# Attention and a tanh-shrink layer on one core: k and q of pairs 8 to 31 turned by the DMA crossbar, loads of two pairs at a time, a new pattern of layer steps

## The chip, the core and the metric

The kernel runs on one core of a Trainium2 chip. Its five engines are PE (TensorE), DVE (VectorE), ACT (ScalarE), POOL (GpSimd) and SP (SyncE, which here issues nearly all DMAs). The metric is the device time of one execution in microseconds, and the number that is compared is the median of several runs.

## The reference

For each of 8 batches and 8 heads there are q, k and v of 576 rows and 64 columns in float32. The rows of the attention's output, with the heads side by side, then pass a layer of two matrix products with `h - tanh(h)` between them.

```python
scores = (1 / sqrt(64)) * q @ k.T
thresh = max(scores, axis=-1) - tau          # tau = 0.02
scores = where(scores >= thresh, scores, -1e9)
attn = softmax(scores)                       # 1e-9 added to the sum
x = (attn @ v), heads side by side           # 4608 x 512
h = x @ w_in                                 # 512 x 2048
out = (h - tanh(h)) @ w_out                  # 2048 x 512
```

## The kernel before, in words

The work goes by pairs of heads: 32 pairs, four to a batch. The two heads of a pair have 1152 rows, cut into 9 tiles of 128 rows of q (`TPP`); there are 288 tiles in all. Eight of a pair's tiles belong to one head; one is shared, 64 rows of each head (`place`, L307).

**Preparing a pair.** `load` (L138) brings k, q and v of a pair from memory, each in two DMAs on SP's queue: rows 0 to 511 of both heads, four consecutive rows to a partition (L145), and the last 64 rows of both heads (L151, L153). `split` (L186, POOL) multiplies by 256 and makes two float16 parts, a high and a low one, side by side, so that a row of 64 becomes 128 columns. `turn` (L253) brings the 128 columns onto the partitions, nine blocks of 128x128: by PE (L240, with `ident_f16` as the moving operand, into the PSUM tile `ps_k` or `ps_q` of the pool `ps_big`, then a DVE copy at L268), or, for q of the pairs that `q_by_dma` (L249) names, by one transposing DMA on SP's queue (L257). Those are pairs 8 and up that are not multiples of 4: 18 pairs. k always goes by PE. `kS` is k with its two halves of 64 partitions swapped, by two POOL copies (L274). `split_v` (L219, POOL) casts v into one of four tiles `vb` that hold a column of ones.

**A tile.** `scores` (L313) does, for each of kT and kS, one matmul of 512 keys and one of 64 keys (L336), into a PSUM tile `psS` of `ps_big`, which has two buffers and is shared with the turns. The shared tile has four times as many, half as wide (L327). DVE scales and takes the row's maximum (L346), then makes the threshold of two tiles (L358). ACT makes z from it (L373): a slope of 1e30 below the threshold stands for the mask. z of two tiles is turned, from pair 6 on by one transposing DMA on SP (L380, tile `zT`), and ACT takes the exponential of both at once (L409, tile `pT`). `attend` (L433 on, L432 and L439; `attend_shared`, L450) multiplies with v; `norm` (L464 on) divides; `emit_x` (L482) turns the result for the layer.

**The layer.** An h step (`hidden`, L501) is four matmuls of 512 columns for one of the 16 blocks of 128 hidden columns; ACT takes the tanh (L518), DVE subtracts (L524). A y step (`project`, L529) is a quarter of one output tile, also four matmuls (L531); after the last quarter a copy (L544) and a store (L547). The halves of the very last tile have tiles `yo` of their own.

**What sets the order.** Nothing is scheduled by a tool: the loop at L730 writes the order down step by step, one step for each tile. In step s it emits the threshold of tile s + 7, the scores of tile s + 8, z (and its turn on SP) of tile s + 5, the tanh of the last h step, the exponential of tile s, the layer step that is due, the rest of the layer, `attend` for tile s - 2 and at last what `plan` holds for the step. Each engine runs its own part of this order and waits where data or a buffer is missing. `PATTERN` (L563) says which layer step a tile's step has: h, y, or none (`-`), in 36 letters for a batch. Batch m's layer runs beside the attention of batch m + 1; the last two batches' layers and the remaining rows end the program alone.

`plan` (L681 on) sets how many steps ahead of a pair's first scores each preparation is emitted: loads 17 to 12, splits 10 to 7, k's turn (with the swap) 6 for most pairs (`k_lead`, L244), v's split 4, q's turn 3, or 7 or 6 by the crossbar. The raw tiles, the float16 parts and kT, kS and qT have two buffers each.

Of the kernel before, what the change touches and what calls it, by code (L numbers as in the profile page):

```python
# [9 lines left out]
F32 = mybir.dt.float32  # L10
BF16 = mybir.dt.bfloat16
FP16 = mybir.dt.float16
# [6 lines left out]
def kernel(  # L19
# [11 lines left out]
    nc = tc.nc  # L31
    P = 128
# [13 lines left out]
    HPAIR = H // 2  # L46
# [85 lines left out]


    raws = {}

    def load(p, t):  # L138
        b, h0 = p // HPAIR, 2 * (p % HPAIR)
        hs = slice(h0, h0 + 2)  # L140
        src = {"k": k, "q": q, "v": v}[t]
        eng = nc.sync
        r = raws[p, t] = raw_pool.tile([P, 10, D], F32, name=f"{t}raw", tag=t)
        n = 8 if t == "v" else 10
        eng.dma_start(  # L145
            out=r[:, 0:n, :].rearrange("p (h c) d -> p h (c d)", h=2)[:, :, 0 : 4 * D],
            in_=src[b, hs, 0:512, :].rearrange("h (p c) d -> p h (c d)", c=4),
        )
        rem = src[b, hs, 512:S, :].rearrange("h s d -> s h d")
        if t == "v":  # L150
            eng.dma_start(out=r[0:64, 8:10, :], in_=rem)  # L151
        else:
            eng.dma_start(out=r[:, 4, :], in_=rem)  # L153

    def load_first(t, h, eng):

        src = {"k": k, "q": q}[t]
        if (0, t) not in raws:
            raws[0, t] = raw_pool.tile([P, 10, D], F32, name=f"{t}raw", tag=t)
        r = raws[0, t]  # L160
        if h is None:
            rem = src[0, 0:2, 512:S, :].rearrange("h s d -> s h d")
            eng.dma_start(out=r[:, 4, :], in_=rem)
        else:
            eng.dma_start(
                out=r[:, 5 * h : 5 * h + 4, :].rearrange("p c d -> p (c d)"),
                in_=src[0, h, 0:512, :].rearrange("(p c) d -> p (c d)", c=4),
            )
# [17 lines left out]
    def split(p, t):  # L186
        x = raws.pop((p, t))[:, 0:9, :]
        hl = hl_pool.tile([P, TPP, 2, D], FP16, name=f"{t}hl", tag=t)
        nc.gpsimd.tensor_scalar(
            out=x, in0=x, scalar1=QKSC, scalar2=1.0, op0=ALU.mult, op1=ALU.mult  # L190
        )
        nc.gpsimd.tensor_copy(out=hl[:, :, 0, :], in_=x)
        nc.gpsimd.tensor_tensor(  # L193
            out=hl[:, :, 1, :], in0=x, in1=hl[:, :, 0, :], op=ALU.subtract
        )
        hls[p, t] = hl
# [21 lines left out]

    def split_v(p):  # L219
        r, vb = raws.pop((p, "v")), vbs[p % NV]  # L220
        nc.gpsimd.tensor_copy(
            out=vb[:, :, 0:4, 0:D],
            in_=r[:, 0:8, :].rearrange("p (h c) d -> p h c d", h=2),
        )
        nc.gpsimd.tensor_copy(out=vb[0:64, :, 4, 0:D], in_=r[0:64, 8:10, :])
        nc.gpsimd.tensor_copy(out=vb[64:P, :, 5, 0:D], in_=r[0:64, 8:10, :])

    mats = {}  # L230


    by_head = lambda ap: ap.rearrange("p (s h) -> p h s", h=2)
    in_heads = lambda ap: ap.rearrange("p (h s) -> p h s", h=2)

    def turn_chunk(out, c, lhsT):
        rhs = ident_f16
        if c == 4:
            out, rhs = in_heads(out), by_head(rhs)
        nc.tensor.matmul(  # L240
            out=out, lhsT=lhsT, rhs=rhs, is_transpose=True, start=True, stop=True
        )
# [4 lines left out]
        return (6, 6)[1 - p % 2]  # L247

    def q_by_dma(p):  # L249

        return p >= 2 * HPAIR and p % 4 != 0

    def turn(p, t):  # L253
        hl = hls.pop((p, t))
        if t == "q" and q_by_dma(p):
            m = mats[p, t] = qk_pool.tile([P, W], FP16, name=f"{t}T", tag=t)
            nc.sync.dma_start_transpose(  # L257
                out=m.rearrange("p (c r) -> p c r", c=TPP),
                in_=hl.rearrange("p c a d -> p (c a d)"),
            )  # L260
            return
        ps = ps_big.tile([P, W], FP16, name=f"ps_{t}", tag="big")
        for c in range(TPP):
            turn_chunk(
                ps[:, c * P : (c + 1) * P], c, hl[:, c, :, :].rearrange("p a d -> p (a d)")
            )
        m = qk_pool.tile([P, W], FP16, name=f"{t}T", tag=t)
        nc.vector.tensor_copy(out=m, in_=ps)  # L268
        mats[p, t] = m
        if t == "k":  # L270
            sw = qk_pool.tile([P, W], FP16, name="kS", tag="ks")
            for lo, hi in ((0, D), (D, 0)):
                o, i = sw[lo : lo + D, :], m[hi : hi + D, :]
                nc.gpsimd.tensor_copy(out=o, in_=i)  # L274
            mats[p, "ks"] = sw

    def turn_first(t, part):

        hl = hls[0, t[0]]
        c0, c1 = ((0, 5), (5, TPP))[part]  # L280
        pl, tag = (ps_y, "y") if t == "ks" else (ps_h, "h")
        ps = pl.tile([P, 5 * P], FP16, name=f"ps1_{t}", tag=tag)
        for c in range(c0, c1):
            o = ps[:, (c - c0) * P : (c - c0 + 1) * P]
            if t == "ks":
                for a in range(2):
                    turn_chunk(o[64 * a : 64 * a + 64, :], c, hl[:, c, 1 - a, :])
            else:
                turn_chunk(o, c, hl[:, c, :, :].rearrange("p a d -> p (a d)"))
        if part == 0:  # L290
            mats[0, t] = qk_pool.tile([P, W], FP16, name=f"{t}T", tag=t)
        dst, n = mats[0, t][:, c0 * P : c1 * P], (c1 - c0) * P
        if part == 1 or t == "q":
            nc.scalar.copy(out=dst, in_=ps[:, 0:n])
        else:
            nc.vector.tensor_copy(out=dst, in_=ps[:, 0:n])


    MAIN = (slice(0, 512), slice(640, W))
    REM = (slice(512, 576), slice(576, 640))  # L300
    scs, mxs, nbs, zs, zts, pts, ops = {}, {}, {}, {}, {}, {}, {}

    def kind(i):
# [9 lines left out]
    def scores(i):  # L313
        p, hh, t = place(i)
        qT, kT, kS = mats[p, "q"], mats[p, "k"], mats[p, "ks"]
        ps = ps_big.tile([P, 1024], F32, name="psS", tag="big")
        main, rem, lo = slice(0, 512), slice(512, 576), 0
        if kind(i) == "B":
            main, rem, lo = slice(512, 1024), slice(448, 512), 448
        if hh is None:  # L320
            qrem = REM
            if q_by_dma(p):
                qrem = (slice(512, 640, 2), slice(513, 640, 2))
            for n, kk in enumerate((kT, kS)):
                for dst, srcs in ((main, MAIN), (rem, REM)):
                    for hh in range(2):
                        nc.tensor.matmul(  # L327
                            out=ps[64 * hh : 64 * hh + 64, dst],
                            lhsT=qT[:, qrem[hh]], rhs=kk[:, srcs[hh]],
                            start=(n == 0), stop=(n == 1),  # L330
                        )
        else:
            lhs = qT[:, (5 * hh + t) * P : (5 * hh + t + 1) * P]
            for n, kk in enumerate((kT, kS)):
                for dst, src in ((main, MAIN[hh]), (rem, REM[hh])):
                    nc.tensor.matmul(  # L336
                        out=ps[:, dst], lhsT=lhs, rhs=kk[:, src],
                        start=(n == 0), stop=(n == 1),
                    )
        sc = sc_pool.tile([P, S], F32, name="sc")  # L340
        if kind(i) == "B":
            mx = mxs[i] = mxs.pop(i - 1)
        else:
            mx = mxs[i] = mx3[i // 2 % len(mx3)]
        c = int(kind(i) == "B")
        nc.vector.tensor_scalar(  # L346
            out=sc, in0=ps[:, lo : lo + S], scalar1=SC, scalar2=None,
            op0=ALU.mult, op1=ALU.max, accum_out=mx[:, c : c + 1],
        )
        scs[i] = sc  # L350
# [163 lines left out]
    def bend():  # L514
        while halves:
            m, n, ps = halves.pop(0)
            th = t_pool.tile([P, MB], F32, name="th")
            nc.scalar.activation(out=th, in_=ps, func=ACT.Tanh)  # L518
            ths.append((m, n, ps, th))

# [8 lines left out]
    def project(m, ms, part, ps, last, cols=slice(0, d_model)):  # L529
# [4 lines left out]
            )  # L534
        if part == 3:
            nc_ = cols.stop - cols.start
            yo = y_pool.tile(
                [P, nc_], F32, name="yo", tag="yo" if nc_ == d_model else f"yo{int(last)}",
                bufs=2 if nc_ == d_model else 1,
            )  # L540
            if last:
                nc.scalar.copy(out=yo, in_=ps)
            else:
# [16 lines left out]
    EARLY = lambda m: 3 if m else 3  # L560
    LAST = 1

    PATTERN = lambda m: '-h--h-hh--h-hh-h-hh-h--hh-h--hh-y-yy' if m == 0 else 'hyhyhyhyhyhyhyhyhyhyhyhyhyhyhyhy' if m == B - 2 else 'yhyhyyy-yhyhhyyhy-hhhyhh-hyhyhy-yhhy'  # L563

    FIRST = 3
    quarters = lambda m: [(m, ms, part) for ms in range(4) for part in range(4)]
# [112 lines left out]
    )  # L679

    plan = {}  # L681
    for p in range(1, NPAIR):
        first = TPP * p - AHEAD
        for d, f in PREP[3 if p == 1 else 0 :]:
            d -= p == 1 and d == 3
# [150 lines left out]
```

## Time and profile before

| | |
|---|---|
| time, median of 3 runs | 518.05 us (518.01 to 518.11) |
| the profiled execution | 518.02 us |
| its span, first to last instruction | 516.2 us |
| granted TensorE clock, mean over the span | 1.000 |
| DMA packets, bytes moved | 208607, 86.79 MB |
| HBM read, written | 36.70 MB, 9.44 MB |
| transposing DMAs | 117 of z, 18 of q |
| PE turns with L240 | 288 matmuls of k, 126 of q (and 18 half ones at the start) |

The page of a profile has the busy time of each engine, the span in 40 slices, the DMA queues, the chain of work that ended last, the costliest groups of instructions, and the DMA issues. Other views list the waits, give the instructions of a stretch in order of time, or the busy times in given stretches. A matmul's duration holds the pipeline's latency; what it costs PE is the distance from its start to the next one's. A PE matmul group in a timeline is several instructions merged: start, time from its first start to its last end, and the count.

### The profile page before, as it was taken

What the parts mean: (1) busy time and instruction counts of PE and PEld (TensorE: products, weight loads), DVE (VectorE), ACT (ScalarE), POOL (GpSimd) and SP (SyncE); (2) the same over time, 40 slices, a digit from 0 to 9 for tenths busy, and PEclk for the clock granted to TensorE, in tenths of its full rate; (3) what the DMA queues carried; (4) which work ended last, traced back from release to release, by engine and by line L of the source; (5) the groups of instructions that cost most, each with busy time, mean ns of one, the idle gap of its engine ahead of it and who ended that gap; (6) DMA issues with size and microseconds to landing.
All of it is one profiled execution on the core that took longest, in us unless ns stands there. A gap on an engine that the chain in (4) does not pass through costs nothing.

```text
span 516.2 us, 12626 instructions
## 1 busy us (share of the span) xinstructions
PE 497.8 (96%) x4540; PEld 285.3 (55%) x4606; DVE 418.8 (81%) x1179; ACT 432.8 (84%) x617; POOL 290.2 (56%) x390
## 2 busy tenths in 40 slices
PE   8999899889999999999999999999999999999997
PEld 4666566555555555555555555555555555544444
DVE  5999889998899988998899888998999887644440
ACT  5999999999899989998999989998999899543430
POOL 8999999776565656566666656566656620000000
PEclk9999999999999999999999999999999999999999
DMA  7852659999999999999999998999989976311013
GB/s 205 259 151 90 205 196 227 165 190 181 193 190 190 207 203 194 187 193 212 201 176 190 197 220 195 183 198 197 203 179 193 172 140 116 97 41 42 20 43 82
DMA packets 208607, 86.79 MB, mean 168 GB/s; under 512 B 176160, under 2 KB 200992, under 8 KB 208544
## 3 DMA queue, kind: packets, MB, share of 16 engines
q1 hardware_dynamic: 207952, 85.56, 80.6%
q8 instruction: 36, 0.59, 0.5%
q10 hardware_dynamic: 592, 0.43, 0.3%
q14 instruction: 27, 0.22, 0.1%
HBM read 36.70 MB, written 9.44 MB: 89 GB/s over the span
## 4 chain that ended last, share of the span: by engine, by line
PE 77%; POOL 9%; ACT 4%; DVE 3%; issue 3%; DMA 2%; SPq 1%; POOLq 0%; ACTq 0%; DVEq 0%
PE psY L531 22%; PE psH L505 19%; PE psS L336 18%; PE psO L439 5%; PE psS L327 3%; PE psHt L505 3%; PE ps_k L240 3%; POOL kS L274 2%; DMA kraw<-in_k_dram 2%; POOL w_in_sb L655 1%; PE psO L450 1%; ACT pT L409 1%; POOL khl L193 1%; PE psO L432 1%; ACT z L373 1%
## 5 line engine op out<-in xcount | busy, mean ns | idle before, releaser
L373 ACT ACTIVATE z<-sc,nb 128x576 bf16<-128x576 f32 x288 | 217.5, 770 | 23.9 <-DVE nb L358 22.2
L346 DVE TENSOR_SCALAR_CACHE_REDUCE sc<-psS 128x576 f32<-128x576 f32 x288 | 213.7, 752 | 17.5 <-PE psS L336 13.3
L531 PE MATMUL psY<-w_out_sb,g 128*128 128x512 bf16 (+1 forms) x565 | 140.2, 373 | 1.3 <-issue 0.2
L409 ACT ACTIVATE pT<-zT 128x1152 f16<-128x1152 bf16 x117 | 134.8, 1152 | 1.7 <-DMA zT<-z 1.4
L274 POOL COPY kS<-kT 64x1152 f16<-64x1152 f16 x62 | 70.7, 1141 | 110.9 <-DVE nb L358 59.6
L505 PE MATMUL psH<-xT,w_in_sb 128*128 128x512 bf16 x443 | 117.8, 379 | 3.5 <-issue 1.1
L336 PE MATMUL psS<-kT,qT 128*128 128x512 f16 (+1 forms) x512 | 104.4, 285 | 4.7 <-DVE sc L346 2.4
L336 PEld LDWEIGHTS <-qT 128*128 128x128 f16 x1024 | 72.9, 97 | 56.5 <-issue 5.5
L524 DVE SCALAR_TENSOR_TENSOR g<-th,psH 128x512 bf16<-128x512 f32 x128 | 87.5, 683 | 18.3 <-ACT th L518 18.0
L336 PE MATMUL psS<-kS,qT 128*128 128x512 f16 x496 | 101.4, 286 | 0.0
L518 ACT ACTIVATE th<-psH 128x512 f32<-128x512 f32 x128 | 74.5, 582 | 20.9 <-PE psH L505 20.9
L531 PEld LDWEIGHTS <-g 128*128 128x128 bf16 x592 | 51.1, 98 | 54.0 <-DVE g L524 0.4
L505 PEld LDWEIGHTS <-w_in_sb 128*128 128x128 bf16 x576 | 49.0, 98 | 56.3 <-issue 3.4
L439 PE MATMUL psO<-vb,pT 128*128 128x65 bf16 x1024 | 53.3, 194 | 0.0
L439 PEld LDWEIGHTS <-pT 128*128 128x128 f16 x1024 | 44.2, 98 | 9.4
L193 POOL TENSOR_TENSOR khl<-kraw,khl 128x576 f16<-128x576 f32 x31 | 39.7, 1280 | 2.6
L193 POOL TENSOR_TENSOR qhl<-qraw,qhl 128x576 f16<-128x576 f32 x31 | 39.7, 1280 | 2.6
L401 ACT ACTIVATE pT<-psZ 128x512 f16<-128x512 bf16 (+1 forms) x54 | 35.1, 654 | 2.2 <-PE psZ L392 1.8
L544 DVE COPY yo<-psY 128x512 f32<-128x512 f32 (+1 forms) x31 | 21.1, 681 | 14.7 <-PE psY L531 13.8
L465 DVE TENSOR_TENSOR osb<-psO,rc 128x256 bf16<-128x256 f32 x64 | 27.2, 424 | 2.2
L432 PE MATMUL psO<-vb,pT 128*128 128x130 bf16 x128 | 28.1, 220 | 0.1
L268 DVE COPY kT<-ps_k 128x1152 f16<-128x1152 f16 x31 | 23.4, 756 | 4.4 <-PE ps_k L240 4.3
(79 smaller groups left out, 509.7 us busy)
## 6 DMA issues: line engine op xcount, KB each, us to landing
vraw<-in_v_dram SPq DMA_DIRECT2D x32, 256.0 KB, 3.4
out_dram<-yo SPq DMA_DIRECT2D x32, 256.0 KB, 2.9
kraw<-in_k_dram SPq DMA_DIRECT2D x31, 256.0 KB, 3.3
qraw<-in_q_dram SPq DMA_DIRECT2D x31, 256.0 KB, 3.4
wt<-in_moe_w_in_dram SPq DMA_DIRECT2D x8, 512.0 KB, 4.6
wt<-in_moe_w_out_dram SPq DMA_DIRECT2D x8, 512.0 KB, 4.0
zT<-z SPq DMA_TRANSPOSE x117, 3.7
qraw<-in_q_dram SPq DMA_DIRECT2D x32, 32.0 KB, 3.1
```

What stands on the lines that cost most here:

```text
L193: nc.gpsimd.tensor_tensor(out=hl[:, :, 1, :], in0=x, in1=hl[:, :, 0, :], op=ALU.subtract)
L274: nc.gpsimd.tensor_copy(out=o, in_=i)
L336: nc.tensor.matmul(out=ps[:, dst], lhsT=lhs, rhs=kk[:, src], start=(n == 0), stop=(n == 1),)
L346: nc.vector.tensor_scalar(out=sc, in0=ps[:, lo : lo + S], scalar1=SC, scalar2=None, op0=ALU.mult, op1=ALU.max, accum_out=mx[:, c : c + 1],)
L373: nc.scalar.activation(out=z, in_=sc, func=ACT.Prelu, bias=nb, scale=1.0, alpha=STEEP)
L401: nc.scalar.activation(out=pt[:, off * P : (off + n) * P], in_=ps[:, 0 : n * P], func=ACT.Exp)
L409: nc.scalar.activation(out=pt[:, 0 : n * P], in_=zts.pop(i)[:, 0:n, :], func=ACT.Exp)
L439: nc.tensor.matmul(out=po[:, t - 1 + ab, :], lhsT=pt[:, blk * P : (blk + 1) * P], rhs=vb[:, hh, c, :], start=False, stop=(n == 7), skip_gr ...
L505: nc.tensor.matmul(out=ps, lhsT=w_in_sb[:, c, n * P : (n + 1) * P], rhs=xs[m][:, c, :] if m < B else xR[:, c, :, :], start=(c == 0), stop= ...
L518: nc.scalar.activation(out=th, in_=ps, func=ACT.Tanh)
L524: nc.vector.scalar_tensor_tensor(out=gs[m][:, n, :], in0=th, scalar=-1.0, in1=ps, op0=ALU.mult, op1=ALU.add,)
L531: nc.tensor.matmul(out=ps, lhsT=gs[m][:, n, ms * P : (ms + 1) * P], rhs=w_out_sb[:, n, cols], start=(n == 0), stop=(n == DF_C - 1),)
```

## The change

From pair 8 on (`DUAL = 8`, the third batch):

- k and q of every pair are turned by a transposing DMA on SP (L291 of the new file), 24 of k and 24 of q; before, 18 of q.
- `load` brings two pairs in one tile. k comes in one DMA, partition p holding rows 9p to 9p + 8 of the pair's 1152 rows, so that one half of the partitions is one head. v comes by rows 9r + c of each head in two DMAs, over the two halves of the partitions. q keeps its rows, one DMA for the four heads and two for the last 64 rows, which now lie head after head.
- The scores read k's columns accordingly: for the 512 keys eight runs of 64 columns out of eight blocks, for the 64 keys one run of the ninth block. The shared tile reads q's columns as two runs of 64 instead of every second column.
- The swap that makes kS is emitted apart from the turn, and a table (`LATER`) sets the leads: an even pair has its loads at 17 (k), 15 (v) and 12 (q), both splits at 9, k's turn at 8, q's at 7, v's split at 4 and the swap at 2; an odd pair has k's split at 12, q's at 11, k's turn at 10, swap and q's turn at 9, and v's split at 3.
- `PATTERN` has another string for batches 1 to 5; those of batches 0 and 6 stay.
- The `yo` halves at the very end take a buffer of the tanh's pool. The raw tiles are twice as large, for all pairs.

On POOL the number and the kinds of instructions are the same; SP has 331 instructions before and 281 after.

```diff
     def load(p, t):
...
+        both = raw_pool.tile([P, 2, 10, D], F32, name=f"{t}raw", tag=t)
+        if p >= DUAL:
+            raws[p, t], raws[p + 1, t] = both[:, 0, :, :], both[:, 1, :, :]
+            rows = src[b, h0 : h0 + 4, :, :]
+            if t == "v":
+                rows = rows.rearrange("h (p c) d -> p h (c d)", c=TPP)
+                dst = both.rearrange("p a (h c) d -> p (a h) (c d)", h=2)
+                eng.dma_start(out=dst[0:64, :, 0 : 4 * D], in_=rows[:, :, 0 : 4 * D])
+                eng.dma_start(out=dst[64:P, :, :], in_=rows[:, :, 4 * D :])
+            elif t == "q":
+                eng.dma_start(
+                    out=both.rearrange("p a (h c) d -> p (a h) (c d)", h=2)[:, :, 0 : 4 * D],
+                    in_=rows[:, 0:512, :].rearrange("h (p c) d -> p h (c d)", c=4),
+                )
+                for a in range(2):
+                    eng.dma_start(
+                        out=both[:, a, 4, :], in_=rows[2 * a : 2 * a + 2, 512:S, :]
+                    )
+            else:
+                eng.dma_start(
+                    out=both[:, :, 0:TPP, :].rearrange("p a c d -> p a (c d)"),
+                    in_=rows.rearrange("(a h) s d -> a (h s) d", a=2).rearrange(
+                        "a (p c) d -> p a (c d)", c=TPP
+                    ),
+                )
+            return
...
     def q_by_dma(p):
-
-        return p >= 2 * HPAIR and p % 4 != 0
+        return p >= DUAL
+
+    def k_by_dma(p):
+        return p >= DUAL
 
     def turn(p, t):
         hl = hls.pop((p, t))
-        if t == "q" and q_by_dma(p):
-            m = mats[p, t] = qk_pool.tile([P, W], FP16, name=f"{t}T", tag=t)
+        if (q_by_dma if t == "q" else k_by_dma)(p):
+            m = mats[p, t] = qk_tile(t)
             nc.sync.dma_start_transpose(
...
         if t == "k":
-            sw = qk_pool.tile([P, W], FP16, name="kS", tag="ks")
...
+            swap(p)
...
+    def main_keys(p, kk, hh):
+        if p < DUAL:
+            return kk[:, MAIN[hh]]
+        return kk[:, 0 : 8 * P].rearrange("p (a n r) -> p n a r", a=2, n=4)[
+            :, :, :, 64 * hh : 64 * hh + 64
+        ]
+
+    def rem_keys(p, kk, hh):
+        return kk[:, 8 * P + 64 * hh : 8 * P + 64 * hh + 64] if p >= DUAL else kk[:, REM[hh]]
...
-    PATTERN = lambda m: '-h--h-hh--h-hh-h-hh-h--hh-h--hh-y-yy' if m == 0 else 'hyhyhyhyhyhyhyhyhyhyhyhyhyhyhyhy' if m == B - 2 else 'yhyhyyy-yhyhhyyhy-hhhyhh-hyhyhy-yhhy'
+    PATTERN = lambda m: '-h--h-hh--h-hh-h-hh-h--hh-h--hh-y-yy' if m == 0 else 'yhyhhyhh-yyhyyhhhyy-hhyyhy-hyhyy-hhy' if m == 1 else 'hyhyhyhyhyhyhyhyhyhyhyhyhyhyhyhy' if m == B - 2 else 'yhyhhyhh-yyhyyhhhyy-hhyyhy-hyhyy-hhy'
...
+    LATER = {
+        0: (
+            ("kt", 8), ("ks", 9), ("vl", 15), ("kl", 17), ("kw", 2),
+            ("ql", 12), ("qs", 9), ("qt", 7), ("vs", 4),
+        ),
+        1: (
+            ("ks", 12), ("qt", 9), ("vs", 3), ("kt", 10), ("qs", 11),
+            ("kw", 9),
+        ),
+    }
```

In `LATER` the first letter names k, q or v; the second letter l is a load, s a split, t a turn and w the swap.

## The prediction

> **What bounds the kernel now.** I read the page's busy shares and the chain that ended last first, then the windows by stage, then the timelines of PE, ACT and SP in one batch, then the DMA issues.
>
> ```profile
> PE 497.8 (96%) x4540; PEld 285.3 (55%) x4606; DVE 418.8 (81%) x1179; ACT 432.8 (84%) x617; POOL 290.2 (56%) x390
> ...
> PE 77%; POOL 9%; ACT 4%; DVE 3%; issue 3%; DMA 2%; SPq 1%; POOLq 0%; ACTq 0%; DVEq 0%
> ```
>
> PE is busy 96% and makes 77% of the chain; POOL's 9% of the chain lies before 65 us. Shares over the whole span hide stages, so here are windows (stretch, its length, then busy us and count by engine): the stretch of pairs 4 to 7 and two steady batches, of four pairs and 36 score tiles each.
>
> ```profile
> core 0: us, PE busy (x) PEld busy (x) DVE busy (x) ACT busy (x) POOL busy (x), PEclk, DMA share, GB/s
> 59.10:114.63 55.53, 50.90 (x550) 32.05 (x559) 49.21 (x142) 51.88 (x80) 47.62 (x61) 1.00 0.84 188
> ...
> 169.46:225.05 55.59, 54.98 (x511) 31.30 (x521) 49.99 (x144) 51.67 (x71) 34.45 (x45) 1.00 1.05 199
> 225.05:280.63 55.58, 54.97 (x510) 31.29 (x521) 49.99 (x144) 51.75 (x71) 34.44 (x45) 1.00 1.08 194
> ```
>
> In a steady batch PE works 54.98 of 55.59 us: what leaves PE there leaves the time. ACT follows with 51.67. In the window before, no engine is full, and PE idles 4.6 us: ACT, DVE and POOL hand the wait around. The granted clock is 1.00 throughout.
>
> **Part 1, the turns that leave PE.** The built orders show 270 fewer 128x128 matmuls: 24 k turns and 6 q turns (pairs 8, 12, ... 28; the other q of pairs 8 to 31 already go by the crossbar), nine each. DVE loses the 30 copies.
>
> ```profile
> 161.91 0.45 PE L450 MATMUL psO<-vb,pT 128*128 128x130 bf16 x5
> 162.20 0.22 PE L432 MATMUL psO<-vb,pT 128*128 128x130 bf16 x1
> ...
> 162.76 0.67 PE L240 MATMUL ps_k<-ident_f,khl 128*128 128x128 f16 x9
> 163.26 0.41 PE L336 MATMUL psS<-kT,qT 128*128 128x512 f16 x2
> ```
>
> The 0.67 holds the pipeline's tail; the next matmul starts 0.50 us after the turn's first, so a turn costs PE 0.50 us. 30 x 0.50 = 15.0 us, 2.5 us a batch. Pair 8's two turns (the k one at 107.4) lie where ACT's timeline, 100 to 114, has one gap of 0.29 us: ACT sets the pace there, and I count them at nothing. **28 x 0.50 = 14.0 us.** PE's wait of psS for DVE's kT copy (1.6 us in all, one of 1.2 at 109.8) goes as well, in that same stretch, and isn't counted. On DVE 30 x 0.756 = 22.7 us go, worth nothing of itself: DVE is 90% busy in a batch and is nobody's last wait there.
>
> **Part 2, what SP gets.** A crossbar transpose holds SP's queue; a load is also issued there.
>
> ```profile
> 174.45 1.32 SPq L257 DMA_TRANSPOSE qT<-qhl  x1
> 175.82 0.79 SPq L145 DMA_DIRECT2D kraw<-in_k_dram  x1
> 176.66 0.60 SPq L153 DMA_DIRECT2D kraw<-in_k_dram  x1
> 177.36 1.50 SPq L380 DMA_TRANSPOSE zT<-z  x1
> ```
>
> Per batch: 5 more transposes at 1.3 us are +6.5; loads go from 24 to 12 (per two pairs one for k, two for v, three for q), 12 x 0.58 = -7.0. SP's sum stays: 21 x 1.3 + 24 x 0.58 + 4 stores x 0.53 = 43.3 us of 55.6 now, 26 x 1.3 + 12 x 0.58 + 4 x 0.53 = 42.9 us of 53.1 after. No row has a load of two pairs; its issue is bounded by 0.38 and 0.79 us, the ends of L145, so 12 of them move SP by at most 2.5 us a batch either way, and SP has 10 spare. SP is in order, and behind each kT and qT stand the zT transposes that ACT's exponentials wait for. In steady state the order has kT, qT, zT in a row once per two pairs: 4.0 us in a period of two steps (one zT, 2.95 us), so that zT is late by 1.1 us, against zT that today, by the timelines, are issued up to 3 us after their z.
>
> Bytes: by the DMA issues zT lands 3.7 us after its issue (median of 117), qT 3.3 (of 18). A transpose moves 128 x 1152 x 2 = 0.295 MB; a batch goes from 11.06 to about 12.5 MB in 53.1 us, 236 GB/s where 199 stands now. Back-to-back transposes ran at 289 GB/s (174.0 to 174.8), loads and stores at 357 (180.0 to 180.6). So the crossbar is not full; landing may grow from 3.7 towards 6.4, the worst zT.
>
> One rule of the skill speaks against this part. The measured row is qT: nine 128x128 blocks land in 3.3 us. The Trainium skill ("VectorE: DVE Perf Modes", The three transpose paths, and its rules) gives 1309 ns a 128x128 block by DMA against 390 ns on TensorE, and advises TensorE wherever PSUM will do. By that page, an estimate, nine blocks take 11.8 us of crossbar, 26 of them 306 us a batch, and the change would be far slower; the same figure would make today's 21 take 247 us of a 55.6 us batch, so the row decides.
>
> **Part 3, kT to kS.** POOL's instructions are the same ones (34.45 us a batch); the swap (2 x 1.14) now waits for a landing instead of a DVE copy. For an even pair kT is issued 8 steps (11.8 us at 1.475 us a step) before its first score; landing 3.7, v's split 1.2 and the odd pair's k split 2.6 partly beside it, swap 2.3: ready some 4 us early. Behind the waiting swap POOL holds the odd pair's q split and swap, which have 5 steps and more. For an odd pair kT must wait until PE has done the last score of the pair two before (two buffers), one step before its issue place; 9 steps remain. By ACT's and DVE's timelines z runs about one step ahead of the score evictions, so SP may stand there up to one step, 1.5 us, with a zT behind it; between zT's landing and its exponential usually lie 2 to 4 us. Cost 0; if that cover is gone, rival B prices it.
>
> **Part 4, k read in runs of 64, v by rows 9r+c.** 480 wide score matmuls read eight runs of 64 columns. Nearest row: the psO matmul of L450 reads two runs of 65, and five of them take 0.29 us, 58 ns each; L432's single run of 130 has the same 220 ns duration. I take 0; the other end is the 3 ns between the two lines' longest (233 and 230), 480 x 3 ns = 1.4 us. Splitting v and the half-width yo in th's buffers change no count: 0, hidden by POOL's 19 idle us a batch and by the tail's PE work.
>
> **Part 5, the pattern.** 16 h, 16 y and 4 empty steps either way; by halves of 18 steps h/y goes from 6/10 and 10/6 to 9/8 and 7/8. It matters through ACT:
>
> ```profile
> 168.51 1.15 ACT L409 ACTIVATE pT<-zT 128x1152 f16<-128x1152 bf16 x1
> 169.56 1.43 ACT L373 ACTIVATE z<-sc,nb 128x576 bf16<-128x576 f32 x2
> 170.89 1.15 ACT L409 ACTIVATE pT<-zT 128x1152 f16<-128x1152 bf16 x1
> ...
> 172.61 0.57 ACT L518 ACTIVATE th<-psH 128x512 f32<-128x512 f32 x1
> 173.09 0.76 ACT L373 ACTIVATE z<-sc,nb 128x576 bf16<-128x576 f32 x1
> ```
>
> Start to start: pT 1.05, z 0.665, th 0.48. A batch's floor on ACT is 36 x 0.665 + 18 x 1.05 + 16 x 0.48 = 50.5 us. PE's batch becomes 55.6 - 2.5 = 53.1, so ACT goes to 95%. By halves (a layer step is 0.86 on PE, the rest 12.8 each): PE 27.4 and 25.7, ACT 25.7 and 24.8, 94% and 96%. Today's second half needs 26.2 of 27.3, 96%, and PE keeps its 99%. So the new pattern fits, by little. I take 0.
>
> **Sum.** The profiled execution is 518.0 us (span 516.2 and 1.8 around it), the same as the median of 518.05. 518.0 - 14.0 = **504.0 us**.
>
> **Rivals.** A: ACT, coupled with DVE, becomes the pace. For it: in 59 to 114 ACT does no better than 51.88 of 55.53, 93.4%, and PE idles. If a batch can't pass that, it takes 51.7 / 0.934 = 55.3 us, 0.3 saved, six batches 1.8: 516.2. Against: part 5's half at 96%. Halfway, 510, is its middle; it spans 506 to 516.
>
> B, the other side: the in-order SP queue. kT of an odd pair stands for PE, its followers are late, zT lands after ACT wants it (today four such waits, 1.4 us in all), and ACT, with 5% to spare, can't catch up. It decides from 14.0 / 12 = 1.2 us lost per two pairs; at 2 us it is 12 x 2 - 14 = +10: 528. Against: SP's sum doesn't grow.
>
> C: the turns only filled time that PE had anyway (its ends are modelled, and the scores' evictions set the pace): 518. Against: from 114 to 420 the waits give PE none of 0.2 us or more on another engine.
>
> **How the numbers follow.** Forecast 60% (its own range 501.0 to 506.0: all 30 turns and the 1.6 us of waits give 501.4; the 1.4 us of part 4 gives 505.4), A 20%, B 15%, C 5%. The range leaves out B and C: 501.0 to 515.0. A change under 0.2% (1.0 us) can't be told from none: A's upper end falls there one time in twenty. Faster 0.79, same 0.06, slower 0.15.
>
> **What would show it.** Right: steady batches near 53.1 us with PE at 99%; no L240 after 105 us; kT landing in 3.3 to 4 us; L274 not ahead of any PE wait. A shows as ACT without gaps and PE waiting for th, g or sc; B as ACT's pT waiting for zT, or PE for kS, with SP standing at kT. Wide scores more than 216 ns apart would break part 4.

## The result, and the profile after

The changed kernel takes 536.6 us (median of 4 runs, 534.46 to 539.94) against 518.06 us: ratio 1.0364, 95% interval 1.0309 to 1.0419. It is slower by 18.5 us where 14 us less was forecast. The profiled run took 537.27 us, with a span of 535.5. Line numbers from here on are the changed kernel's, unless an experiment is named: zT L428, the turns by crossbar L291, pT L457, the swap to kS L313, score matmuls L384.

The page of the changed kernel, engine shares, DMA by slice, and the chain that ended last:

```profile
PE 494.3 (92%) x4336; PEld 272.2 (51%) x4336; DVE 398.3 (74%) x1149; ACT 433.3 (81%) x617; POOL 292.4 (55%) x390
...
DMA  7744659999999999999999999999999996401113
...
PE 27%; DMA 22%; POOL 20%; ACT 15%; issue 8%; DVE 5%; SPq 1%; POOLq 0%; ACTq 0%; DVEq 0%
```

PE lost work but fell from 77% of the chain to 27%; DMA, 2% before, is 22%. Two steady batches of four pairs, cut at every 36th z (ACT's mask instruction, one for each score tile; stretch, length, busy us and count by engine, clock, DMA share, GB/s):

```profile
core 0: us, PE busy (x) PEld busy (x) DVE busy (x) ACT busy (x) POOL busy (x), PEclk, DMA share, GB/s
134.47:193.80 59.33, 54.85 (x483) 29.60 (x482) 46.69 (x139) 51.76 (x72) 33.77 (x44) 1.00 1.07 205
193.80:252.60 58.80, 53.61 (x468) 28.93 (x466) 46.45 (x139) 51.61 (x72) 34.81 (x44) 1.00 1.11 209
```

A batch takes 59 us instead of 55.6. No compute engine is full in it: ACT works 51.6 of 58.8 us and PE at most 54.9. Bytes moved at 205 to 209 GB/s, hardly above the 194 to 199 of before and far from the 236 that the forecast needed. The waits (who waited for what: us in total, times, the longest):

```profile
POOL qraw L216 <- DMA qraw<-in_q_dram: 77.4, 12, 7.5
DVE g L572 <- ACT th L566: 72.4, 70, 2.9
ACT pT L457 <- DMA zT<-z: 35.0, 33, 2.6
...
PE psS L384 <- POOL kS L313: 13.3, 11, 2.3
```

ACT's wait for zT was 1.4 us, four times, before. SP's timeline shows why zT is late:

```profile
198.57 1.37 SPq L428 DMA_TRANSPOSE zT<-z  x1
200.04 1.24 SPq L594 DMA_DIRECT2D out_dram<-yo  x1
201.38 2.87 SPq L428 DMA_TRANSPOSE zT<-z  x1
204.30 0.57 SPq L154 DMA_DIRECT2D qraw<-in_q_dram  x1
204.93 1.16 SPq L159 DMA_DIRECT2D qraw<-in_q_dram  x2
206.19 4.45 SPq L428 DMA_TRANSPOSE zT<-z  x2
210.75 1.32 SPq L291 DMA_TRANSPOSE kT<-khl  x1
```

Each row begins within 0.1 us or so of the last one's end: SP has no idle time. The transpose at 201.38 holds SP for 2.87 us and the first of the two at 206.19 for 3.06, behind the loads of k (194.67), v (196.91) and q (204.30); their z had ended 2.7 and 2.9 us before they began. Over the whole run, before (L380) and after (L428), the shortest, median and longest hold in ns of a zT row were:

```profile
L380 SPq DMA_TRANSPOSE zT<-z x117: 1242/1477/2679, 80.6 to 439.8; - x117
...
L428 SPq DMA_TRANSPOSE zT<-z x117: 1242/1402/3730, 80.7 to 459.2; - x117
```

The shortest row is the same and the median even fell; the loss is in the long rows, and the mean rose from 1.55 to 1.80 us. The chain in the same stretch is made of zT transposes (5 to 6 us from issue to landing, where the median before was 3.7), of q's load, and after it of some 9 us of POOL's splits and swaps, up to PE's scores:

```profile
194.57 0.77 ACT pT L457
195.34 6.00 DMA zT<-z
...
204.93 4.27 DMA qraw<-in_q_dram
...
217.48 1.15 POOL kS L313
...
218.68 0.41 PE psS L384 x2
...
223.60 0.86 ACT pT L457
224.46 5.14 DMA zT<-z
```

So there are two suspects, SP's queue and POOL's line; the experiments separate them.

SP's rows can be added up. Over the whole run SP issued 382 DMAs before, 135 of them transposes, and 340 after, with 165 transposes (the 331 and 281 given with the change are not what the traces have). The table adds up the rows of the kernels on which the argument rests, over the same work, four steady batches (144 score tiles, from the 91st z on), with "rest" for the time that no transpose and no other DMA instruction (loads, stores) takes up. The rest holds the gap of some 0.1 us between any two rows, so it doesn't fall to zero when the queue is full. A mean over 1.27 us, which is near the shortest row, is called stretch; that transfers already under way cause it is tested by thin_loads below.

| kernel | time, us | four batches | transposes: number, us, mean | other DMAs: number, us | rest |
|---|---|---|---|---|---|
| before | 518.0 | 222.3 | 84, 129.5, 1.54 | 114, 68.0 | 24.8 |
| after | 537.3 | 236.2 | 104, 178.8, 1.72 | 63, 41.8 | 15.6 |
| k_on_pe | 527.2 | 227.5 | 88, 151.5, 1.72 | 64, 39.6 | 36.3 |
| dummy | 549.1 | 244.4 | 104, 155.0, 1.49 | 111, 71.7 | 17.7 |
| sp_issues | 542.2 | 242.5 | 84, 125.2, 1.49 | 152, 96.2 | 21.1 |
| plain_dummy | 528.7 | 230.5 | 84, 125.6, 1.50 | 133, 86.7 | 18.2 |
| thin_loads | 508.7 | 214.6 | 104, 158.6, 1.53 | 63, 40.2 | 15.8 |
| single | 539.2 | 238.4 | 105, 162.2, 1.54 | 96, 60.4 | 15.8 |
| early | 540.0 | 237.3 | 103, 171.3, 1.66 | 64, 47.6 | 18.4 |
| loads_on_pool | 564.3 | 252.9 | 104, 215.3, 2.07 | 16, 10.5 | 27.1 |
| loads_on_act | 560.5 | 252.1 | 105, 197.7, 1.88 | 16, 9.5 | 44.9 |
| early_half | 535.6 | 234.6 | 96, 160.2, 1.67 | 64, 44.1 | 30.3 |
| early_pe | 524.6 | 226.2 | 84, 152.3, 1.81 | 64, 40.8 | 33.1 |
| k_rows | 518.2 | 222.3 | 84, 131.4, 1.56 | 96, 57.7 | 33.2 |
| k_rows_q | 515.4 | 220.3 | 88, 135.3, 1.54 | 96, 56.3 | 28.7 |

### The profile page after: what moved, and what is told of

Read it like the earlier page. It is cut to its first block, busy times and chain, and to the rows that moved or that the text cites. A ratio compares the mean times of both kernels' runs of the same rounds, so it can differ in the third digit from the quotient of the medians.

```text
span 535.5 us, 12081 instructions
## 1 busy us (share of the span) xinstructions
PE 494.3 (92%) x4336; PEld 272.2 (51%) x4336; DVE 398.3 (74%) x1149; ACT 433.3 (81%) x617; POOL 292.4 (55%) x390
## 4 chain that ended last, share of the span: by engine, by line
PE 27%; DMA 22%; POOL 20%; ACT 15%; issue 8%; DVE 5%; SPq 1%; POOLq 0%; ACTq 0%; DVEq 0%
DMA zT<-z 16%; PE psY L579 10%; PE psH L553 8%; ACT z L421 7%; POOL kS L313 6%; ACT pT L457 5%; PE psS L384 4%; DMA qraw<-in_q_dram 4%; ACT th L566 3%; POOL khl L220 3%; PE psHt L553 3%; DVE g L572 2%; POOL kraw L216 2%; POOL khl L219 1%; POOL vb L249 1%
## 5 line engine op out<-in xcount | busy, mean ns | idle before, releaser
L457 ACT ACTIVATE pT<-zT 128x1152 f16<-128x1152 bf16 x117 | 135.5, 1158 | 35.2 <-DMA zT<-z 35.0
L579 PE MATMUL psY<-w_out_sb,g 128*128 128x512 bf16 (+1 forms) x592 | 146.6, 375 | 0.0
L553 PE MATMUL psH<-xT,w_in_sb 128*128 128x512 bf16 x480 | 123.3, 379 | 6.5 <-DVE g L572 6.1
L384 PE MATMUL psS<-kS,qT 128*128 128x512 f16 (+1 forms) x512 | 104.9, 287 | 13.3 <-POOL kS L313 13.3
L384 PEld LDWEIGHTS <-qT 128*128 128x128 f16 x1024 | 74.1, 98 | 72.5 <-issue 18.0
L384 PE MATMUL psS<-kT,qT 128*128 128x512 f16 (+1 forms) x512 | 104.8, 286 | 2.7 <-DVE sc L394 1.7
L313 POOL COPY kS<-kT 64x1152 f16<-64x1152 f16 x62 | 70.9, 1143 | 24.7 <-DMA kT<-khl 14.8
L553 PEld LDWEIGHTS <-w_in_sb 128*128 128x128 bf16 x576 | 49.4, 97 | 61.6 <-issue 9.7
L216 POOL TENSOR_SCALAR qraw<-qraw 128x576 f32<-128x576 f32 x31 | 20.8, 672 | 78.5 <-DMA qraw<-in_q_dram 77.4
L216 POOL TENSOR_SCALAR kraw<-kraw 128x576 f32<-128x576 f32 x31 | 20.8, 672 | 23.6 <-DMA kraw<-in_k_dram 22.3
L591 DVE COPY yo<-psY 128x512 f32<-128x512 f32 (+1 forms) x31 | 21.1, 679 | 12.7 <-PE psY L579 12.4
```

What stands on the lines that cost most here:

```text
L216: nc.gpsimd.tensor_scalar(out=x, in0=x, scalar1=QKSC, scalar2=1.0, op0=ALU.mult, op1=ALU.mult)
L384: nc.tensor.matmul(out=ps[:, dst], lhsT=lhs, rhs=cols(p, kk, hh), start=(n == 0), stop=(n == 1),)
L457: nc.scalar.activation(out=pt[:, 0 : n * P], in_=zts.pop(i)[:, 0:n, :], func=ACT.Exp)
L553: nc.tensor.matmul(out=ps, lhsT=w_in_sb[:, c, n * P : (n + 1) * P], rhs=xs[m][:, c, :] if m < B else xR[:, c, :, :], start=(c == 0), stop= ...
L579: nc.tensor.matmul(out=ps, lhsT=gs[m][:, n, ms * P : (ms + 1) * P], rhs=w_out_sb[:, n, cols], start=(n == 0), stop=(n == DF_C - 1),)
```

## The experiments

All but the last two are single runs; the changed kernel's own four spread over 5.5 us, so only larger differences are read. T1 is the theory that more transposes go to the transfers than these can carry, so that zT is late (rival B's mechanism); T2, that POOL, which works in order, stands for loads and makes kS late. A third suspect is the pattern. X, Y and Z are finer forms of T1.

**k_on_pe: the k turns back on PE.**

```
     def k_by_dma(p):
-        return p >= DUAL
+        return False
```

> k goes back to PE (24 turns, 24 fewer transposing DMAs); loads of two pairs, leads, pattern and the 24 crossbar turns of q stay. Theory 1, the transfers: 30 more transposes and big loads back up the DMA queue, so zT and kT land late; then this comes to about 515 (518.0 less six q turns of 0.50), and ACT's wait for zT falls from 35.0 us to under 10. Theory 2, POOL's line: POOL stands 7 us per two pairs at q's split, because the load of two pairs' q is late, and kS waits behind it; the swap is still behind q's split here, so the time stays near 530 and POOL's wait for qraw near 77 us. Theory 3, the pattern: stays above 530.

527.2 us, and ACT's wait for zT falls to 6.9 us. Half of the loss goes with 24 transposes. It is still 9 us over before, which T1 alone did not say: SP's rest is 36.3 us here, so its queue is not full, and POOL has 25% of the chain, against 9% before. What makes these 9 us was not tested apart.

**pool_order: POOL's splits at other steps, so that PE does not wait for kS.**

```
-("ql", 12), ("qs", 9),  ...  ("ks", 12),
+("ql", 12), ("qs", 8),  ...  ("ks", 18),
```

> Only POOL's order changes: the odd pair's k split moves ahead of the even pair's q split (leads 12 to 18 and 9 to 8), so POOL works in the 7 us in which it stood, and kS is ready some 2.7 us earlier. Theory 2: PE's 13.3 us of waits for kS go, 524. Theory 1: the waits for kS go too, but ACT's 35 us of waits for zT stay and the time falls by less than 6, 531 or more. Theory 3: no change, 537.

538.0 us. PE's waits for kS all but went (0.9 us), the time stayed; ACT waited 37.2 us for zT. POOL's part of the chain is back at the 9% of before:

```profile
PE 37%; ACT 22%; DMA 18%; POOL 9%; issue 8%; DVE 5%; SPq 0%; ACTq 0%; POOLq 0%
```

T2's wait is real but not what sets the end.

**old_pattern: the pattern of before in batches 1 to 5.**

> The changed kernel with the pattern of before for batches 1 to 5. Theory 3, the new pattern's crowded h steps make ACT late: 525 or less. Theories 1 and 2: within 4 us of 537, either side.

539.7 us: the old pattern wins nothing back, so the new one is not the cause.

**dummy: before, plus 30 transposes that nobody reads.** PE keeps its turns.

```
+        if p >= 2 * HPAIR:
+            spare = qk_pool.tile([P, W], FP16, name="spare", tag="spare")
+            nc.sync.dma_start_transpose(out=spare..., in_=hl...)
```

> The kernel before, with 30 transposing DMAs added whose result nobody reads (the k turns from pair 8 on and the six q turns of PE, at the place of each turn); PE still does its turns, loads are those of before. Theory 1: crossbar work by itself delays zT: 525 to 540, ACT's wait for zT from 1.4 us to 10 or more. Theory 2 and 3: 518 to 520, since POOL's line and the pattern are those of before.

549.1 us: 31.0 us more, 1.03 us a transpose, from transposes alone. The waits of this kernel:

```profile
ACT pT L415 <- DMA zT<-z: 43.9, 24, 3.5
```

A turn on PE cost 0.50 us. Exchanging one for the other loses 0.53 us, 30 times 16 us: most of the 18.5, if the change of the loads comes to nothing; the run "single" below shows that it does.

**thin_loads: the loads bring a quarter of their bytes.** Each SP instruction stays; the rest of each tile keeps old values, so the kernel leaves out part of the computation.

```
-out=dst[0:64, :, 0 : 4 * D], in_=rows[:, :, 0 : 4 * D]
+out=dst[0:64, :, 0:D], in_=rows[:, :, 0:D]          (v; q and k likewise)
```

> The changed kernel, whose q, k and v loads of the pairs from 8 on bring about a quarter of their bytes (64 of 256 columns for q and v, 128 of 576 for k; the rest of each tile holds old values, and the scaling of these pairs is by 1, so part of the computation is left out). The number of SP's instructions, of transposes and of every engine's work stays. Theory X, the DMA engines are full: about 2.6 of 12.5 MB a batch go, at the 203 GB/s that the dummy run sustained 49 us a batch, under PE's 53, so 504 to 512 us. Theory Y, SP's queue is full by the time of its issues, whatever they move: 530 to 538 us.

508.7 us, and PE is busy for 98 to 99% of a batch again:

```profile
core 0: us, PE busy (x) PEld busy (x) DVE busy (x) ACT busy (x) POOL busy (x), PEclk, DMA share, GB/s
134.71:188.84 54.13, 53.10 (x471) 28.78 (x468) 46.46 (x139) 51.37 (x71) 33.04 (x43) 1.00 1.04 172
188.84:242.66 53.82, 53.07 (x472) 28.87 (x470) 46.74 (x139) 51.21 (x71) 34.74 (x44) 1.00 1.03 182
```

With the loads' bytes gone, the stretch falls from 1.72 to 1.53 us a transpose (20 us in four batches) and the changed kernel does nearly what was forecast: 53.8 us a batch where 53.1 were forecast. X's number is met. The SP queue is no emptier (rest 15.8), it only takes less time for the same rows, so bytes act through the time for which each transpose holds SP.

**sp_issues: before, plus 60 DMAs of 128 bytes on SP.**

```
+            for n in range(2):
+                nc.sync.dma_start(out=spare[0:1, 64 * n : 64 * n + 64], in_=hl[0:1, 0, n, :])
```

> The kernel before, with two DMAs of 128 bytes on SP ahead of each of the 30 turns that stay on PE (their target is never read): 60 more instructions in SP's queue and next to no bytes. Theory Y, SP's issues are the limit: 60 x some 0.55 us = 33 us, so 545 to 551 us. Theory X, the DMA engines are the limit: 518 to 522 us.

542.2 us: 24.2 us more, 0.40 us for each instruction that moves next to nothing. X falls; Y came near. ACT waits for zT here too:

```profile
ACT pT L413 <- DMA zT<-z: 32.9, 23, 3.3
```

**plain_dummy: before, plus 30 plain copies of the dummy's tiles.**

> The kernel before, with 30 plain copies of the same 288 KB tiles inside SBUF (no transpose) where the dummy run had 30 transposes; nothing reads them. If the DMA engines' bytes are the limit, whatever the path: as the dummy run, 545 to 550 us. If it is a rate of the transposing path alone: 518 to 525 us. If SP's issue time: 30 x some 0.55 us = 17 us at most, 530 to 535 us.

528.7 us: 10.7 us more, 0.36 us each, the same as a 128-byte DMA. 8.85 MB more, at 217 GB/s in a steady batch, cost no more than as many DMAs of 128 bytes. So the 205 to 209 GB/s of the changed kernel is no ceiling of the DMA engines for every kind of transfer, and a transpose costs about three times what a copy of the same tile does.

These three answer together. X alone would leave sp_issues at 518, Y alone would leave thin_loads at 530. From here Z: SP's queue in order is the pace, and its load is the instructions plus the stretch by what is in flight.

**dual_only: all 30 turns back on PE, two-pair loads and the rest kept.**

```
-        return p >= DUAL                    (q_by_dma)
+        return p >= DUAL and p % 4 != 0
-        return p >= DUAL                    (k_by_dma)
+        return False
```

> The changed kernel with all 30 turns back on PE (k of every pair, q of every fourth), so that only the loads of two pairs, the row order and the pattern of layer steps are left of the change. Theory X: the same bytes and transposes as before, 518 to 522 us. Rival, large loads of two pairs stand in front of the zT and cost by themselves: the run with k on PE was 9 us over before with six transposes more, which by the dummy run's 1.03 us each are 6; the other 3 would be here, 521 us or more. Theory Y: fewer load instructions on SP, 515 to 518 us.

544.2 us, which none of the theories gave. It is a fault of the experiment, not a full queue (SP's rest is 57.6 us in four batches): the steps of the changed kernel leave q's load three steps before its split, POOL stands for it, and a turn on PE now waits for POOL (a turn by crossbar did not stop PE):

```profile
POOL qraw L216 <- DMA qraw<-in_q_dram: 83.7, 12, 8.4
...
PE ps_q L272 <- POOL qhl L220: 14.3, 6, 3.7
```

These 14.3 us are about half of the 26 by which the run is over before; the other half was not followed up.

**spread: the changed kernel with its loads six steps apart** (k 20, q 14, v 8 steps ahead for 17, 12, 15).

> The changed kernel with its loads of two pairs set six steps apart (k 20, q 14 and v 8 steps ahead instead of 17, 12 and 15); nothing else moves. Theory Z, SP's queue is full, and what fills it beside the issues is the time by which transposes stretch behind clumped loads (46.7 us over 1.27 us each in four batches here, 22.9 in the kernel before): the stretch falls toward 28 us, four batches to 215 to 222 us, 514 to 522 us in all. Rival, the bytes as such are too many: 532 to 538 us, as the changed kernel.

582.8 us, a miss of the same sort: v now lands after its split's step, and kS waits in POOL's line behind it.

```profile
POOL vb L249 <- DMA vraw<-in_v_dram: 67.8, 9, 8.2
...
PE psS L384 <- POOL kS L313: 53.5, 12, 6.4
```

It says nothing on the cause, but gives the price of a load that is too late; the stretch did not fall either (180.7 us of transposes in four batches).

**loads_on_pool, loads_on_act: the two-pair loads issued by another engine.**

```
-        eng = nc.sync
+        eng = nc.gpsimd if p >= DUAL else nc.sync      (nc.scalar in the other)
```

> The changed kernel with the loads from pair 8 on issued by POOL in place of SP: the same bytes at the same steps, but some 42 us of load instructions in four batches leave SP's queue. Theory Z: SP's sum falls from 236 to about 194 us in four batches, under PE's 212, so 504 to 515 us, if POOL's own queue (it stands for q already) bears them. Rival, the DMA engines' bytes: 530 to 538 us. A loss of more than that would be POOL's, by waits there that hold the loads back.

> The changed kernel with the loads from pair 8 on issued by ACT in place of SP: same bytes, same steps; 12 issues of some 0.6 us in two pairs go from SP to ACT. Theory Z: SP is relieved by 10 us a batch, but ACT's 50.5 us a batch become some 58 to 61 (a load may stand behind the full DMA rings there too): 522 to 540 us, with ACT at over 85% and the waits for zT down to the 1 to 5 us of before. Rival, the bytes: the waits for zT stay at some 35 us and the time is 535 us or more.

564.3 and 560.5 us. SP got rid of some 30 us of instructions in four batches, and its transposes took 36 and 19 us more. SP's timeline with the loads on POOL, where POOL issued k, v and q from 205.45 to 211.3:

```profile
203.94 3.91 SPq L428 DMA_TRANSPOSE zT<-z  x2
207.96 0.97 SPq L594 DMA_DIRECT2D out_dram<-yo  x1
209.35 16.15 SPq L428 DMA_TRANSPOSE zT<-z  x3
225.60 1.37 SPq L291 DMA_TRANSPOSE kT<-khl  x1
```

Three transposes hold SP for 16.15 us while loads of another queue are in flight. So the stretch does not need the loads in SP's own queue, and Z's "194 us" was wrong: it took away the instructions and forgot that the transfers stay. The Trainium skill ("DMA: Bandwidth & Descriptors", Issuing engines are not separate DMA queues) says that issuing from several engines only saves the issue time, "which is usually small relative to the DMA itself". These two runs agree with the first half: with the issue moved, the transfers and what they hold up were still there. For one DMA the second half holds here too: in sp_issues a DMA of 128 bytes held SP for 0.59 us on average and landed 2.1 to 2.3 us after its issue (medians). Added up in a full queue it is not small: 60 of them cost 24 us. SP did have idle time in these two runs (rest 27.1 and 44.9), so its sum is not what set their times. With the loads on POOL, ACT stood 58.0 us for zT; what set the time with the loads on ACT was not worked out.

**spread_pe: dual_only with later turns on PE, loads six steps apart.**

> The dual_only kernel (all 30 turns on PE) with the loads six steps apart as in the spread run, k's even turn two steps after its split instead of one, and q's turns on PE four steps ahead, as the kernel before has them, instead of seven and nine: dual_only's waits of PE for the split of k and q go. The loads of two pairs then stand alone. Theory Z: PE is full as in the kernel before, SP has 25 us less of load instructions in four batches: 516 to 520 us. Rival, loads of two pairs cost by themselves: 525 us or more.

528.5 us: the rival's number, but POOL still stands 65.2 us for q's load, so it doesn't separate the two.

**single: the changed kernel with each pair loading its own.** The row order and all 48 crossbar turns stay.

```
-            rows = src[b, h0 : h0 + 4, :, :]
+            rows = src[b, h0 : h0 + 2, :, :]
```

> The changed kernel with each pair loading its own k, q and v (288 KB a load instead of 576), in the same row order; the odd pair's loads at 20, 18 and 14 steps ahead of its first step, the even pair's where they were. All 48 turns stay on the crossbar. Theory Z, SP's queue sets the pace: the loads' instructions go from 42 to some 66 us in four batches, while the transposes' stretch falls from 0.45 us each to the 0.22 to 0.27 of the runs with loads of one pair (104 x 0.2 = 21 us): no change within some 6 us, 531 to 543 us. Rival, loads of two pairs are the loss: back to 515 to 522 us.

539.2 us, the time of the changed kernel. The two-pair loads save 18.6 us of load instructions in four batches and give back 16.6 us as stretch. They are neither the loss nor a gain here.

**early: the changed kernel with its loads at 20 (k), 19 (q) and 14 (v) steps.**

> The changed kernel with its even pairs' loads issued at 20 (k), 19 (q) and 14 (v) steps ahead instead of 17, 12 and 15, so that POOL's 77 us of standing for q go. Theory Z: SP's queue has the same instructions and stays full, 530 to 540 us, though POOL no longer stands. Rival, POOL's standing for q holds up kS and the splits and is the loss: 505 to 520 us.

540.0 us. POOL's 77 us of standing for q are gone from the waits (41.0 for v came instead), PE's waits for kS are 1.2 us in all, the time is not better, and ACT waits on:

```profile
ACT pT L457 <- DMA zT<-z: 40.8, 19, 4.1
```

With pool_order this rules T2 out.

**early_pe and early_half: those loads, with all 30 turns on PE, and with only 12 (k of the even pairs) on PE.**

> The loads of two pairs alone: all 30 turns on PE (where the kernel before has them), loads at 20, 19 and 14 steps ahead, k's even turn three steps after its split, q's turns on PE four steps ahead. Theory Z: SP is not full (some 30 us less of load instructions, 17 more of stretch) and PE is, as in the kernel before: 515 to 520 us. Rival, large loads cost by themselves: 525 us or more, with PE waiting.

> As early_pe, but q of all pairs and k of the odd pairs on the crossbar: 12 turns more than the kernel before, 18 fewer on PE... of the 30 turns that the change takes off PE, 18 go and 12 (k of the even pairs) stay. Theory Z: SP's sum in four batches is 96 transposes x 1.72 + 41 + some 14 = 220 us against PE's 215: 514 to 519 us. Rival, every transpose over the 84 of before costs its 1.03 us as in the dummy run and returns 0.50: 518 + 18 x 0.53 = 527 us.

524.6 and 535.6 us. Z missed both. With two-pair loads and no turn moved the kernel is 6.5 us over before, though SP's rest in four batches is 33.1 us, the same as in k_rows below (33.2), which loses nothing; ACT's wait for zT is 19.5 us in early_pe:

```profile
212.90 4.17 SPq L428 DMA_TRANSPOSE zT<-z  x2
217.12 0.70 SPq L163 DMA_DIRECT2D kraw<-in_k_dram  x1
217.87 0.48 SPq L154 DMA_DIRECT2D qraw<-in_q_dram  x1
218.40 1.17 SPq L159 DMA_DIRECT2D qraw<-in_q_dram  x2
219.66 3.98 SPq L428 DMA_TRANSPOSE zT<-z  x1
```

One zT behind the loads of k and q holds SP for 3.98 us (the longest in that run 4.7; in k_rows_q 2.3). So SP's sum over a batch is not the whole test: single late zT can hurt where the mean has room. The price of a turn agrees with the dummy's: from early_pe to early 30 turns go to the crossbar (some at other steps), +15.4 us and 15.0 off PE, 1.01 us each.

**k_rows: before with the row order alone, a pair at a time.** k comes in one DMA, v by rows 9r + c in two (its lines are left out here), the score matmuls read runs of 64.

```
+        if p >= ROWS and t == "k":
+            eng.dma_start(
+                out=r[:, 0:TPP, :].rearrange("p c d -> p (c d)"),
+                in_=src[b, hs, :, :].rearrange("h s d -> (h s) d").rearrange(
+                    "(p c) d -> p (c d)", c=TPP))
+            return
```

> The kernel before with one part of the change alone: k and v of the pairs from 8 on by rows 9r+c, a pair at a time, so that k comes in one DMA instead of two and its columns reach the score matmuls in runs of 64; turns, steps and pattern are those of the kernel before. SP has 24 instructions less (each of the 60 more in the sp_issues run cost 0.40 us), PE the same work. If PE is the bound of the kernel before: 516 to 518.5 us. If runs of 64 columns cost PE the 0.06 us a step that the prediction bounded: up to 14 us more. If SP's queue was the bound of the kernel before: 24 x 0.40 = 10 us less, 508 us.

518.24 us (ratio 1.0002, 0.9992 to 1.0011). No gain and no cost: PE is the bound, and 24 fewer DMAs only add to SP's rest (24.8 to 33.2 us in four batches). In the changed kernel's trace too, score matmuls of eight runs of 64 columns start 216 ns apart, as those of 512 columns did before.

**k_rows_q: that, and q of every pair from 8 on by the crossbar.**

```
-        return p >= 2 * HPAIR and p % 4 != 0
+        return p >= 2 * HPAIR
```

> The k_rows kernel with q of every pair from 8 on turned by the crossbar: 6 turns more than in the kernel before, 6 x 0.50 = 3 us less of PE. With SP's 24 instructions (some 10 us by the sp_issues run) gone and 6 x 1.03 us of transposes come back, SP has room for them: 513 to 517 us, the best of all versions. If every transpose over the 84 of four batches of the kernel before costs its 1 us whatever else leaves the queue: 519 to 521 us.

515.40 us (ratio 0.9947, 0.9932 to 0.9962): 0.5% under before, with the whole interval below 1, and the least of all versions that compute the result. Its page, engine shares, chain and ACT's row for pT (busy us, mean ns, idle before):

```profile
PE 494.4 (96%) x4486; PEld 282.1 (55%) x4552; DVE 415.9 (81%) x1173; ACT 432.8 (84%) x617; POOL 291.5 (57%) x390
...
PE 75%; POOL 9%; ACT 5%; issue 3%; DVE 3%; DMA 2%; SPq 1%; POOLq 0%; ACTq 0%; DVEq 0%
...
L442 ACT ACTIVATE pT<-zT 128x1152 f16<-128x1152 bf16 x117 | 134.8, 1152 | 0.0
```

A steady batch of it, columns as in the windows above:

```profile
187.92:243.00 55.08, 54.47 (x500) 30.81 (x508) 49.53 (x143) 51.65 (x70) 34.70 (x44) 1.00 1.04 206
```

ACT never waits for zT, PE is at 99% of the batch, and six turns give 2.8 us over k_rows, 0.47 each of the 0.50 that PE's rows promised. With loads of one pair and room in SP's queue these crossbar turns cost nothing; in dummy and early, without it, 1.0 us each.

## Why the prediction was wrong

The step that failed is Part 2: "SP's sum stays: ... 43.3 us of 55.6 now, ... 42.9 us of 53.1 after", and "SP has 10 spare". The term with the wrong size is the transposes' time. The forecast let it grow by 6.5 us a batch against 7.0 us of loads saved; measured, it grew by 12.3 us (129.5 to 178.8 us in four batches) against 6.6 saved. Its 1.3 us a transpose fits the rows of qT (mean 1.36 us over the run of before) but not those of zT, 117 of the 135, whose mean was 1.55; and it was taken to stay the same with more transposes and larger loads, while the mean over both kinds went from 1.54 to 1.72. The 0.58 us for a load was near the mean of 0.60 (the 0.79 given as L145's longest row holds for one batch; between 114 and 420 us it is 1.45). The gaps between rows were left out, 4 to 6 us a batch.

So SP was at 49.4 us of 55.6 a batch already before and came to 55.2 of 59.0. Where SP is the pace, 16 to 21 us of four batches were left over in every run, so of the 24.8 before only some 4 to 9 were free. The prediction had a sign of it in hand: zT "issued up to 3 us after their z" had been standing in SP's line. By the simplest count, an estimate, single's 21 more transposes at 1.54 us are 32 us; k_rows leaves 33 less 16, 17 us free; 15 remain, and single's four batches are 16 us longer than those of k_rows.

A second reading of that part is not borne out: "So the crossbar is not full", from 289 and 357 GB/s in bursts of a microsecond. In the changed kernel's steady batches only 205 to 209 passed. plain_dummy's 217 shows that it isn't one limit in bytes; a stream's rate in a burst of one kind does not say what a mixture holds.

The other steps:

- **Part 1**, 0.50 us of PE a turn: right (0.47 in k_rows_q). Where the transfers allow it, 9.3 of the 14.0 us come: thin_loads gives 508.7, with batches of 53.8 to 54.1 us (forecast 53.1) and PE at 53.1 of them.
- **Part 3**, kS "ready some 4 us early": wrong; PE waited for kS 11 times, 13.3 us, since q's load of two pairs lands late and POOL stands for it up to 7.5 us ahead of the swap. It is on the chain, but not what decides: pool_order and early took most of those waits away for nothing.
- **Part 4**, runs of 64 free: right (k_rows, 1.0002; 216 ns from start to start).
- **Part 5**, the pattern: not the cause (old_pattern), though a cost of it on PE or ACT could not show while SP is the pace. ACT did not become the pace (51.6 of 58.8 us), so rival A is out, and so is C: thin_loads and k_rows_q were quicker by PE's turns.
- **Rival B** named the mechanism, the in-order SP queue with zT late, and had 15%. "Against: SP's sum doesn't grow" is the same failed term. Its place was wrong as well: not a kT that stands for PE (kT's rows held SP for 1.34 us at the median, 2.08 at most), but the zT transposes themselves, each held up by what is in flight. Its 528 was too low.

What stays open: why k_on_pe loses 9 us with 36 us of SP's rest, why early_half loses 17.6 us with 30 us of SP's rest, and how much of that is single late zT and how much POOL (its swap waited 93.3 us there for kT's copy). That loads of two pairs make single transposes long is seen; that this is the whole of early_pe's 6.5 us is argued, not shown. Whether the stretch arises in the transposing path or in the queues ahead of it, no run separates. By the count above, an estimate, the k_rows kernel should bear more crossbar turns than the six of k_rows_q; that was not tried.

## What to carry to other kernels

Before work is moved to the DMA queue, add up the durations of all rows of the issuing engine over a steady stretch, gaps too, and not a short row times the count. Here 11% seemed to be left before (24.8 of 222.3 us), and most of that could not be used. A transfer's price is what it holds up in its queue, so first free places there (one DMA for two, as k's rows did), and then move only as many operations as fit. Large loads need not save what their fewer instructions promise if a short transfer that others wait for stands behind them: here they saved 18.6 us of instructions and gave back 16.6.

## What the runs showed of the hardware that was not expected

- A nine-block transpose (128x1152, 0.295 MB) held SP for 1.24 us at least, 1.5 on average among loads of 256 to 288 KB, 1.66 to 1.81 among loads of up to 576 KB, and 8.9 at most while another engine's loads were in flight (loads_on_pool).
- A DMA of 128 bytes and a copy of 288 KB inside SBUF cost about the same in SP's full queue, 0.40 and 0.36 us; a transpose of the same 288 KB cost 1.03. The Trainium skill ("DMA: Bandwidth & Descriptors", Latency and other measured facts) gives 261 GB/s as the effective rate of DMA transposes with a non-contiguous middle dimension, and some 350 to 400 for the contiguous case; estimates from them, 0.295 MB at these rates, are 1.13 and 0.74 to 0.84 us. The price lies between; no run here shows which case holds.
- Loads moved from SP to POOL or ACT made the changed kernel 28 and 24 us slower, though three quarters of SP's load and store time in the steady batches had left it.
- A matmul's moving operand in eight runs of 64 columns took the time of one run of 512 (k_rows).
